# Block 0's loads split over two queues, and the tables, gathers and weight loads around the last blocks reordered, in a retention and mixture-of-experts kernel

## The chip, the cores and the metric

The kernel runs on one core of a Trainium2 chip. The metric is the device time of one execution in microseconds (us), the median of several runs; lower is better. TensorE is called PE here (its weight loads PEld), VectorE is DVE, ScalarE is ACT, GpSimd is POOL and SyncE is SP. DMAs are issued by the queues of SP, ACT and POOL.

## What is computed

The reference has two stages. The first is a retention layer over q, k and v of shape (4, 8, 768, 64); its output, seen as 3072 tokens of 512 numbers, is the input x of the second, a mixture of 8 experts in which each token goes to one expert.

```python
for t in range(S):
    state = gamma[None, :, None, None] * state + np.einsum('bhd,bhe->bhde', k[:, :, t], v[:, :, t])
    y[:, :, t] = scale * np.einsum('bhd,bhde->bhe', q[:, :, t], state)
...
xn = x / (np.linalg.norm(x, axis=-1, keepdims=True) + 1e-06)
en = expert_emb / (np.linalg.norm(expert_emb, axis=-1, keepdims=True) + 1e-06)
logits = xn @ en.T / tau
expert_idx = np.argmax(logits, axis=1)
...
for e in range(E):
    mask = expert_idx == e
    h = np.maximum(x[mask] @ w1[e], 0.0)
    out[mask] = gate_w[mask, None] * (h @ w2[e])
```

## The kernel before

**Blocks.** The retention runs in 12 blocks `m` of 256 tokens. A block's q and k are scaled (`scale_q`, `scale_k`), transposed on PE (`transpose_q`, `transpose_k`), and copied from PSUM by ACT. `scores` makes the products of q and k, `masks` (DVE) takes them out of PSUM, `state` adds k and v to the running state, and `inter` and `intra` make the output; `take` (ACT) copies it, `rows_turn` (DVE) transposes it and `rows` (SP) writes it to the table `xd` in HBM. The order of every engine's instructions is the order of the program text; each queue is in order.

**Start.** Block 0's q comes in two loads and its k in two halves of four heads, all issued by SP (L327, L322). PE meanwhile multiplies zeros (`W0`, L725). DVE scales block 0; later blocks are scaled by POOL.

**Routing.** `expert_emb` is a generator of four steps: load the embeddings `em` and `tau`, start the norm, finish it, transpose to `enT`. Its steps are spread over the starts of blocks 0 to 2. From block 3 on, `logits_products` and `logits_rows` make the logits of finished blocks into a tile called `parts`; `em` and the constant tile `none`, which fills the slot table `tbl` (L834), carry the same name and share two buffers with it. The groups of `GROUPS` finish after blocks 2, 5, 7, 8, 10 and 11: `sums`, `choose` and `add_counts` find each token's expert, `count` and `ranks` its slot, and `place` (POOL, L566) writes its row into `tbl`, one indirect DMA for each 128 tokens. `pad` raises the first expert's count after the fourth group.

**Weights.** `load_piece` (SP) loads 512 KB of weights into one of four `raw` buffers, `split_cast` (ACT, L219) makes the high part, and its `low` (DVE, L224) the low part. The first expert's first four pieces are loaded around blocks 8 and 9 (`LOADS`, and two more at the top of block 9, each piece in four DMAs) and split at the end of block 9 and the top of block 10.

**Hand-over.** In block 10 `early_slots` loads the first 288 slots of expert 0, `early_gather` turns them into indices (`indices`, L590) and fetches their rows (L596) into `xge`. After block 11 PE starts the first expert's layer (`run(n)` makes `n` products of it); the last 128 slots of expert 0 are loaded at L937 and fetched into `xr0` (L1081), which `turn_late` transposes (L1094). The other experts follow one by one.

Of the kernel before, what the change touches and what calls it, by code (L numbers as in the profile page):

```python
# [24 lines left out]
P = 128  # L25
# [28 lines left out]
LOADS = (8, 8)  # L54
# [14 lines left out]
W0 = 10  # L69
# [36 lines left out]
def retention_moe(ctx: ExitStack, tc: tile.TileContext, q, k, v, emb, tau, w1, w2, const, const16, out):  # L106
# [213 lines left out]
    def load(dst, src, m, h=slice(0, H)):  # L320
        b, c = divmod(m, NCB)
        return nc.sync.dma_start(out=dst[:, h], in_=src[b, h, c * T2:(c + 1) * T2, :].rearrange("h (p s) d -> p h s d", s=2))  # L322

    def load_q(m):
        b, c = divmod(m, NCB)
        src = q[b, :, c * T2:(c + 1) * T2, :].rearrange("(j a) (t s) d -> a t j (s d)", a=2, s=8)
        return [nc.sync.dma_start(out=qin[m % 3][:, a], in_=src[a]) for a in range(2)]  # L327

    def load_k(m, h=slice(0, H)):
        return load(kin[m % 3], k, m, h)  # L330
# [21 lines left out]
    def copy_k(m, s, ps, copy=nc.scalar.copy):  # L352
        if m not in kTs:
            kTs[m] = ap_.tile([P, KT, 2, 2, 64], F32, name="kT")
        return copy(out=kTs[m][:, :, :, s], in_=ps.rearrange("p (j u c) -> p j u c", j=KT, u=2))  # L355
# [233 lines left out]
    def indices(p, e, c):  # L589
        nc.gpsimd.tensor_scalar(out=gi[:p, e, c], in0=tb[:p, e, c, 0], scalar1=float(NT - 1), scalar2=None, op0=ALU.min)  # L590

    def tokens(p, e, c):
        nc.gpsimd.tensor_copy(out=si[:p, e, c], in_=tb[:p, e, c, 1])

    def gather(xr, n, j, e, at, rows_=NT):
        return nc.gpsimd.indirect_dma_start(  # L596
            out=xr[:n, j, :], out_offset=None, in_=xd[:rows_, :],
            in_offset=bass.IndirectOffsetOnAxis(ap=gi[:n, e, at:at + 1], axis=0),
            bounds_check=rows_ - 1, oob_is_err=False)
# [124 lines left out]
    for _ in range(W0):  # L724
        nc.tensor.matmul(idle, zeros[:, :P], zeros, start=True, stop=True)  # L725
# [13 lines left out]
    nc.gpsimd.memset(none, float(NONE))  # L739
# [22 lines left out]
    for m in range(NM):  # L762
        nxt = m + 1 < NM
        done = last_of.get(m - 1)
        if waiting is not None:
            pr = count(waiting)
            if span(waiting).stop == NBE:
                pad()
            run_all(ranks(waiting, pr))
            ready += range(span(waiting).start, span(waiting).stop)  # L770
        py_of(m)
        if m == NM - 2:
            first, lows = lows, [split_cast(), split_cast()]
            for u in range(2):
                spread_v(m + 1, u)

        for u in range(2):
            o = masks(scores(m, u), u)
            if u == 0:
                i = o[0]  # L780
        n = 2 if m < 7 else 3 if m < 9 else 4
        if m == NM - 2:
            place(ready)
            ready = []
        if m == 0:
            for j in (*load_q(2), load_k(2)):
                after(j, i)
            nc.sync.dma_start(out=cst2, in_=const[:, _C1:])
            nc.sync.dma_start(out=tri, in_=const16)

        if m + 2 < NM:
            for s in range(2):
                after(scale_k(m + 2, s), i)
            for s in range(2):
                after(scale_q(m + 2, s), i)
        if m == 2:
            nc.gpsimd.tensor_copy(out=zt[:, :, :2], in_=C("ids").rearrange("p (n o) -> p n o", o=2))
# [11 lines left out]
        if m == 0:  # L809
            state(0)  # L810
            state_copy(0)
            state_sums(0)
            intra(0, 0)
# [12 lines left out]
        else:  # L826
# [10 lines left out]
            for i in () if m < 3 else (0, 1, 2) if m == 3 else (m - 1,):  # L837
                logits_rows(i, logits_products(i))
            if nxt:
# [7 lines left out]
                transpose_k(m + 1, 1)  # L847
                rows(m - 1, gathered if m == NM - 2 else None)
                if m == NM - 2:
                    for low in first:  # L850
                        low()
                    load_piece(gathered)
                    load_piece(gathered)
                if done is not None:
# [18 lines left out]
        if m == NM - 3:  # L873
            lows = [split_cast(), split_cast()]
# [3 lines left out]
        if m < 3:  # L878
# [56 lines left out]
    load_expert(1)  # L935
    load_expert(2)
# [3 lines left out]
    run(10)  # L940
    split()
# [6 lines left out]
    for _ in range(4):  # L948
        load_piece()
# [130 lines left out]
    indices(P, 0, slice(3, 4))  # L1080
    gather(xr0, P, 0, 0, 3)  # L1081
# [186 lines left out]
    with ExitStack() as cx:  # L1268
# [3 lines left out]
        def expert_rows(e, i):  # L1272
# [10 lines left out]
            nc.vector.tensor_scalar(out=g1, in0=mt[:, :1], scalar1=float(NT - 1), scalar2=None, op0=ALU.min)  # L1283
            nc.vector.tensor_copy(out=s1, in_=mt[:, 1:2])
# [26 lines left out]
        with tc.If(any_over > 0):  # L1311

            none = op.tile([P, SW], F32, name="none")
            nc.gpsimd.memset(none, float(NONE))
# [39 lines left out]
```

## Time and profile before

| | us |
|---|---|
| median of 3 runs (402.48 to 404.23) | 403.92 |
| the profiled execution | 404.24 |
| its span | 402.5 |
| PE busy | 386.1 |
| DVE busy | 254.1 |
| ACT busy | 213.4 |
| POOL busy | 150.9 |

The span runs from the first to the last recorded instruction; 1.7 us of the profiled execution lie outside it. Times in the rows count from the span's start. A stage is told by its start and end on this scale: the blocks run from about 10 to 118 us, the experts from about 120 us to the end.

### The profile page before, as it was taken

The numbers are of one execution on the slowest core, as the hardware profiler recorded it, in microseconds if no ns is written. First come the engines' busy times: TensorE is split into PE (matmuls) and PEld (weight loads), VectorE is DVE, ScalarE is ACT, GpSimd is POOL, SyncE is SP. The second block draws the span as 40 slices with busy tenths as digits, with TensorE's granted clock in tenths as the row PEclk, the third lists the DMA queues.
The fourth block names the chain that finished last, engine by engine and source line by source line (L and its number), as shares of the span: only waits on it lengthen the run. The fifth ranks groups of instructions, "written<-read, shape, count | busy, mean of one in ns | idle before, by whom it ended". The sixth has DMA issues, their size and how long they took to land.

```text
span 402.5 us, 9525 instructions
## 1 busy us (share of the span) xinstructions
PE 386.1 (96%) x3646; PEld 355.2 (88%) x3646; DVE 254.1 (63%) x539; ACT 213.4 (53%) x378; POOL 150.9 (37%) x171
## 2 busy tenths in 40 slices
PE   6999999999899999999999999999999999999993
PEld 3998788887779978999999999999889889999972
DVE  5497867877889638854863864757456456485400
ACT  3575557565945356555544736725665445463410
POOL 2575487687445522402502611420371062001131
PEclk9999999999999999999999999999999999999998
DMA  7899979889448779589879797787888977933121
GB/s 228 262 287 254 277 225 280 235 229 260 104 130 258 234 263 265 161 267 249 266 223 247 241 302 175 246 277 221 236 273 298 190 240 225 246 122 107 31 99 54
DMA packets 88479, 88.41 MB, mean 220 GB/s; under 512 B 10803, under 2 KB 66995, under 8 KB 88424
## 3 DMA queue, kind: packets, MB, share of 16 engines
q1 hardware_dynamic: 83176, 74.60, 65.4%
q0 software_dynamic: 5072, 13.05, 9.6%
q8 instruction: 30, 0.49, 0.5%
q14 instruction: 25, 0.20, 0.2%
q10 hardware_dynamic: 176, 0.07, 0.1%
HBM read 65.01 MB, written 18.79 MB: 208 GB/s over the span
## 4 chain that ended last, share of the span: by engine, by line
PE 62%; DMA 15%; DVE 7%; issue 5%; SPq 5%; POOL 2%; ACT 2%; POOLq 0%; DVEq 0%
PE pst L237 10%; PE b L237 8%; PE py L1024 8%; PE py L237 8%; PE b L1024 5%; DMA xd<-x 5%; PE pst L1024 4%; PE b L1072 4%; PE py L1072 4%; DMA wlo<-in_k_dram 3%; SPq L1036 2%; DVE x L468 2%; PE b L381 2%; DMA xr<-xd,gi 2%; SPq L475 2%
## 5 line engine op out<-in xcount | busy, mean ns | idle before, releaser
L224 DVE TENSOR_TENSOR wlo<-raw,whi 128x1024 fp32r<-128x1024 f32 x64 | 77.8, 1218 | 23.2 <-ACT whi L219 18.3
L1054 POOL DMA_INDIRECT out_dram<-og,si x28 | 29.3, 1047 | 119.0 <-ACT og L1047 84.2
L219 ACT CAST whi<-raw 128x1024 fp32r<-128x1024 f32 x64 | 66.3, 1044 | 4.7 <-DMA raw<-in_moe_w_dram 4.6
L596 POOL DMA_INDIRECT xr<-xd,gi x25 | 29.3, 1171 | 17.5 <-issue 15.1
L401 DVE TENSOR_TENSOR pm<-b,mask 128x512 f32<-128x512 f32 x48 | 29.8, 681 | 8.9 <-PE b L381 8.9
L344 POOL TENSOR_TENSOR hl<-wlo,cst 128x512 f32<-128x512 f32 x22 | 22.6, 1049 | 31.5 <-DMA wlo<-in_k_dram 17.4
L237 PE MATMUL pst<-xl,whi 128*128 128x380 f32 (+7 forms) x96 | 32.1, 335 | 0.0
L237 PE MATMUL pst<-xh,whi 128*128 128x380 f32 (+7 forms) x96 | 32.0, 334 | 0.0
L237 PE MATMUL pst<-xh,wlo 128*128 128x380 f32 (+7 forms) x96 | 32.0, 333 | 0.0
L1005 DVE STREAM_TRANSPOSE xt<-xg 128x384 f32<-128x384 f32 (+1 forms) x28 | 15.7, 578 | 25.8 <-DMA xg<-xs 25.7
L263 POOL TENSOR_TENSOR r<-r,half 128x4 f32<-128x4 f32 (+1 forms) x9 | 8.9, 991 | 54.1 <-DVE r L262 54.1
L566 POOL DMA_INDIRECT tbl<-zt,sloti x24 | 24.2, 1009 | 12.6 <-issue 5.4
L243 ACT ACTIVATE hh<-pst 128x380 fp32r<-128x380 f32 (+7 forms) x24 | 11.6, 485 | 31.6 <-PE pst L237 31.6
L381 PE MATMUL b<-qT,kT 64*128 64x128 f32 x384 | 24.9, 279 | 2.4 <-ACT kT L355 1.5
L1006 ACT CAST xh<-xt 128x408 fp32r<-128x408 f32 (+6 forms) x28 | 14.2, 510 | 24.1 <-DVE xt L1005 23.8
L237 PE MATMUL b<-xh,whi 128*128 128x408 f32 (+7 forms) x80 | 26.7, 334 | 0.0
L237 PE MATMUL b<-xl,whi 128*128 128x408 f32 (+7 forms) x80 | 26.7, 333 | 0.0
L237 PE MATMUL b<-xh,wlo 128*128 128x408 f32 (+7 forms) x80 | 26.6, 332 | 0.0
L237 PE MATMUL py<-xh,whi 128*128 128x288 f32 (+7 forms) x80 | 26.3, 329 | 0.0
L237 PE MATMUL py<-xh,wlo 128*128 128x288 f32 (+7 forms) x80 | 26.2, 328 | 0.0
L237 PE MATMUL py<-xl,whi 128*128 128x288 f32 (+7 forms) x80 | 26.2, 327 | 0.0
L381 PEld LDWEIGHTS b<-qT,kT 64*128 64x128 f32 x384 | 22.5, 188 | 3.9 <-ACT kT L355 2.8
(220 smaller groups left out, 1044.2 us busy)
## 6 DMA issues: line engine op xcount, KB each, us to landing
raw<-in_moe_w_dram SPq DMA_DIRECT2D x60, 512.0 KB, 4.4
whi<-in_q_dram SPq DMA_DIRECT2D x24, 256.0 KB, 4.0
xd<-x SPq DMA_DIRECT2D x48, 128.0 KB, 4.2
wlo<-in_k_dram SPq DMA_DIRECT2D x11, 512.0 KB
xs<-xr SPq DMA_DIRECT2D x6, 768.0 KB, 4.8
whi<-in_v_dram SPq DMA_DIRECT2D x6, 512.0 KB
wlo<-in_v_dram SPq DMA_DIRECT2D x6, 512.0 KB, 6.0
xg<-xs SPq DMA_DIRECT2D x16, 192.0 KB, 4.6
```

What stands on the lines that cost most here:

```text
L219: nc.scalar.copy(out=hv, in_=rv)
L224: eng.tensor_tensor(out=lv, in0=rv, in1=hv.bitcast(F32), op=ALU.subtract)
L237: nc.tensor.matmul(acc[:, :w], a[:, f], x[:, kt, cols], start=(n == 0), stop=(n == 3 * KT - 1))
L344: return eng.tensor_tensor(out=ks_r[:, m % 3, s, h], in0=kin[m % 3][:, h, s], in1=w[:, h], op=ALU.mult)
L381: nc.tensor.matmul(psc[a][:, j], kTs[m][a * D:(a + 1) * D, j, u].rearrange("p s c -> p (s c)"), q_cols(m, a, j, u), start=True, stop=True, ...
L401: o.append(nc.vector.tensor_tensor(out=pm, in0=psc[a], in1=w, op=ALU.mult))
L566: i = nc.gpsimd.indirect_dma_start(out=tbl[:, :], out_offset=bass.IndirectOffsetOnAxis(ap=sloti[:, n:n + 1], axis=0), in_=zt[:, n], in_off ...
L596: return nc.gpsimd.indirect_dma_start(out=xr[:n, j, :], out_offset=None, in_=xd[:rows_, :], in_offset=bass.IndirectOffsetOnAxis(ap=gi[:n, ...
L1005: nc.vector.transpose(out=xt[:, :n], in_=xgs[e][:, :n, kt * Q:(kt + 1) * Q])
L1024: nc.tensor.matmul(acc[:, :c], a[:, f], x[:, kt, :c], start=(n == 0), stop=(n == 3 * FT - 1))
L1054: i = nc.gpsimd.indirect_dma_start(out=out[:, :], out_offset=bass.IndirectOffsetOnAxis(ap=si[:n, e, j:j + 1], axis=0), in_=og[:n, j, :], i ...
L1072: nc.tensor.matmul(acc[:s, :], x[:, kt, at], a, start=(n == 0), stop=(n == 3 * FT - 1))
```

## The change

- q and k of block 0: one half is issued by SP, the other by ACT behind `cst1`, in front of the embedding loads.
- Warming products: 12 in place of 10 at the start, then `fill` adds one, three and one between the transposes of block 0; their bank is `py0`. `copy_k` of block 0 copies each half for itself.
- The embedding chain: all steps after the loads in block 0. The logits begin in block 2 (blocks 0 and 1), then one block each.
- The slot table holds integers; `early_gather` and the gather of `xr0` take their indices from `tb` as loaded, without `indices`. `xr0` is set to zero by POOL first.
- Weight pieces 0 to 3: two at the end of block 7, two at the end of block 8; split at the end of blocks 8 and 9. Their low parts stay in blocks 10 and 11, the first of them earlier in block 10.
- Block 9: `sums`, `choose`, `add_counts` come before the transposes of `rows`. Block 10: `ranks` before `pad`.
- `scale_q` of block 11 moves from block 9 to block 10, behind `place` and in front of the early gather.
- After block 11: the next expert's first two pieces are issued in front of L937 and the slot loads of experts 1 and 2; two follow at the old place, where there were four.

```diff
-LOADS = (8, 8)
+LOADS = (7, 7, 8, 8)
-W0 = 10
+W0 = 12
...
     def early_gather():
-        indices(P, 0, slice(0, 3))
         for j, n in EROWS:
-            i = gather(xge, n, j, 0, j, NBE * P)
+            i = gather(xge, n, j, 0, j, NBE * P, tb[:n, 0, j, :1].bitcast(I32))
         tokens(P, 0, slice(0, 3))
...
-    idle = pt_()
+    idle = bank("py0")
     halves = [slice(0, H // 2), slice(H // 2, H)]
     nc.scalar.dma_start(out=cst1, in_=const[:, :_C1])
-    load_q(0)
-    for h in halves:
-        load_k(0, h)
+    load_q(0, (nc.sync, nc.scalar))
+    for h, eng in zip(halves, (nc.sync, nc.scalar)):
+        load_k(0, h, eng)
...
+    def fill(n):
+        for _ in range(n):
+            nc.tensor.matmul(idle, zeros[:, :P], zeros, start=True, stop=True)
+
+    fill(W0)
...
     transpose_q(0, 1)
+    fill(1)
     kps = [pt_(), pt_()]
     for i, h in enumerate(halves):
+        js = slice(2 * i, 2 * i + 2)
         for s in range(2):
             scale_k(0, s, nc.vector, h)
         for s in range(2):
             turn_k(0, s, kps[s], range(2 * i, 2 * i + 2))
-    copy_k(0, 0, kps[0])
-    copy_k(0, 1, kps[1], nc.vector.tensor_copy)
+        fill(1 if i else 3)
+        copy_k(0, 0, kps[0], js=js)
+        copy_k(0, 1, kps[1], nc.vector.tensor_copy if i else nc.scalar.copy, js)
...
+            run_all(ranks(waiting, pr))
             if span(waiting).stop == NBE:
                 pad()
-            run_all(ranks(waiting, pr))
...
         if m == NM - 2:
-            first, lows = lows, [split_cast(), split_cast()]
...
+        if m == 0:
+            next(emb_steps)
...
             place(ready)
             ready = []
+            for s in range(2):
+                scale_q(m + 1, s)
...
-            for s in range(2):
+            for s in range(2 if m < NM - 3 else 0):
                 after(scale_q(m + 2, s), i)
...
-        if m == NM - 3:
-            load_piece()
-            load_piece()
...
             state_sums(0)
+            next(emb_steps)
...
-            for i in () if m < 3 else (0, 1, 2) if m == 3 else (m - 1,):
+            if m == NM - 2:
+                lows.pop(0)()
+            for i in () if m < 2 else (0, 1) if m == 2 else (m - 1,):
...
+                if m == NM - 3:
+                    z = sums(done)
+                    run_all(choose(done, z))
+                    run_all(add_counts(done))
                 rows(m - 1, gathered if m == NM - 2 else None)
...
         if m == NM - 3:
-            lows = [split_cast(), split_cast()]
+            lows += [split_cast(), split_cast()]
         take(m)
...
+        if m == NM - 4:
+            lows = [split_cast(), split_cast()]
-        if m < 3:
+        if m == 0:
             next(emb_steps)
...
     load_expert(1)
+    load_piece()
+    run(10)
+    split()
+    load_piece()
     load_expert(2)
     nc.sync.dma_start(out=tb[:, 0, 3], in_=tbl[EARLY:CAPS[0], :2 + NE])
     slots(1)
     slots(2)
-    run(10)
-    split()
     run(12)
...
-    for _ in range(4):
-        load_piece()
+    load_piece()
+    load_piece()
...
-    indices(P, 0, slice(3, 4))
-    gather(xr0, P, 0, 0, 3)
+    nc.gpsimd.memset(xr0, 0.0)
+    gather(xr0, P, 0, 0, 3, idx=tb[:, 0, 3, :1].bitcast(I32))
```

## Rows read from the trace of the kernel before

**Rows 1.** The page, part 1: busy us, share of the span, instructions.

```profile
PE 386.1 (96%) x3646; PEld 355.2 (88%) x3646; DVE 254.1 (63%) x539; ACT 213.4 (53%) x378; POOL 150.9 (37%) x171
```

**Rows 2.** Busy time of each engine in stretches of the span; the first line names the columns.

```profile
core 0: us, PE busy (x) PEld busy (x) DVE busy (x) ACT busy (x) POOL busy (x), PEclk, DMA share, GB/s
0.00:10.00 10.00, 6.53 (x30) 3.16 (x32) 5.21 (x9) 3.76 (x6) 2.60 (x19) 1.00 0.80 227
...
143.50:395.00 251.50, 251.50 (x1360) 238.92 (x1361) 147.51 (x290) 130.97 (x230) 65.16 (x67) 1.00 0.73 216
...
84.00:92.00 8.00, 7.55 (x166) 6.58 (x157) 6.24 (x20) 5.48 (x10) 5.96 (x6) 1.00 0.84 245
```

**Rows 3.** PE's waits from 20 to 165 us: total, times, longest.

```profile
PE b L535 <- DVE oh L526: 2.7, 5, 0.7
...
PE py L444 <- DVE vs L394: 0.4, 1, 0.4
```

**Rows 4.** Timeline of the start: start us, us, engine, line, operation, [idle before].

```profile
0.80 1.33 SPq L327 DMA_DIRECT2D whi<-in_q_dram  x2
...
1.25 3.62 PE L725 MATMUL b<-x 128*128 128x512 bf16 x10 [1.25 <-DVE x L706]
...
2.17 1.14 SPq L322 DMA_DIRECT2D wlo<-in_k_dram  x2
...
5.90 1.06 PE L368 MATMUL b<-ident,hh 128*128 128x128 f32 x8 [1.03 <-DVE hh L339]
...
7.20 1.69 PE L350 MATMUL b<-ident,hl 128*128 128x128 f32 x8 [0.23 <-DVE hl L344]
...
7.63 0.76 DVE L344 TENSOR_TENSOR hl<-wlo,cst 128x256 f32<-128x256 f32 x2 [0.15 <-DMA wlo<-in_k_dram]
...
9.76 2.06 PE L381 MATMUL b<-qT,kT 64*128 64x128 f32 x32 [0.88 <-DVE kT L355]
```

**Rows 5.** Timeline of DVE in block 3.

```profile
41.25 1.11 DVE L496 STREAM_TRANSPOSE parts<-b 128x256 f32<-128x256 f32 x3 [1.93 <-DMA tbl<-parts]
```

**Rows 6.** Timeline of SP, POOL, ACT and PE in blocks 8 to 11.

```profile
86.07 0.54 SPq L322 DMA_DIRECT2D wlo<-in_k_dram  x1
...
92.31 8.33 SPq L192 DMA_DIRECT2D raw<-in_moe_w_dram  x16
...
92.53 2.04 POOL L344 TENSOR_TENSOR hl<-wlo,cst 128x512 f32<-128x512 f32 x2 [1.80 <-DMA wlo<-in_k_dram]
...
99.59 0.17 PE L535 MATMUL b<-oh,tri 128*128 128x16 f16 x1 [0.67 <-DVE oh L526]
...
100.22 1.05 ACT L219 CAST whi<-raw 128x1024 fp32r<-128x1024 f32 x1 [0.98 <-DMA raw<-in_moe_w_dram]
...
103.18 0.97 POOL L566 DMA_INDIRECT tbl<-zt,sloti  x1 [0.30 <-issue]
...
106.01 1.04 PE L368 MATMUL b<-ident,hh 128*128 128x128 f32 x8
106.14 2.50 ACT L394 COPY vs<-wlo 64x512 f32<-64x512 f32 x4
...
108.89 0.95 POOL L590 TENSOR_SCALAR gi<-tb 128x3 int32<-128x3 f32 x1 [4.74 <-DMA tb<-tbl]
...
110.83 2.06 PE L381 MATMUL b<-qT,kT 64*128 64x128 f32 x32 [1.45 <-ACT kT L355]
```

**Rows 7.** Timeline of SP, POOL and PE after block 11.

```profile
132.24 0.35 SPq L937 DMA_DIRECT2D tb<-tbl  x1
...
133.98 1.12 POOL L590 TENSOR_SCALAR gi<-tb 128x1 int32<-128x1 f32 x1 [5.57 <-DMA tb<-tbl]
134.06 2.18 SPq L194 DMA_DIRECT2D raw<-in_moe_w_dram  x4
...
135.37 1.14 POOL L596 DMA_INDIRECT xr<-xd,gi  x1 [0.28 <-DMA tb<-tbl]
...
143.47 0.66 PE L1094 MATMUL b<-ident,xr 128*128 128x128 f32 x4 [0.99 <-DMA xr<-xd,gi]
```

More of the change, by code (lines that the diff above doesn't have):

```diff
@@ L318, in retention_moe, with load, load_q, load_k @@
     xge = ap_.tile([P, len(EROWS), DM], F32, name="xge", bufs=1)
-    def load(dst, src, m, h=slice(0, H)):
+    def load(dst, src, m, h=slice(0, H), eng=nc.sync):
         b, c = divmod(m, NCB)
-        return nc.sync.dma_start(out=dst[:, h], in_=src[b, h, c * T2:(c + 1) * T2, :].rearrange("h (p s) d -> p h s d", s=2))
-    def load_q(m):
+        return eng.dma_start(out=dst[:, h], in_=src[b, h, c * T2:(c + 1) * T2, :].rearrange("h (p s) d -> p h s d", s=2))
+    def load_q(m, engs=(nc.sync, nc.sync)):
         b, c = divmod(m, NCB)
         src = q[b, :, c * T2:(c + 1) * T2, :].rearrange("(j a) (t s) d -> a t j (s d)", a=2, s=8)
-        return [nc.sync.dma_start(out=qin[m % 3][:, a], in_=src[a]) for a in range(2)]
-    def load_k(m, h=slice(0, H)):
-        return load(kin[m % 3], k, m, h)
+        return [engs[a].dma_start(out=qin[m % 3][:, a], in_=src[a]) for a in range(2)]
+    def load_k(m, h=slice(0, H), eng=nc.sync):
+        return load(kin[m % 3], k, m, h, eng)
     def load_v(m, h=slice(0, H)):
@@ L350, in turn_k, with copy_k @@
             nc.tensor.transpose(ps[:, j * P:(j + 1) * P], ks_r[:, m % 3, s, 2 * j:2 * j + 2], ident)
-    def copy_k(m, s, ps, copy=nc.scalar.copy):
+    def copy_k(m, s, ps, copy=nc.scalar.copy, js=slice(0, KT)):
         if m not in kTs:
             kTs[m] = ap_.tile([P, KT, 2, 2, 64], F32, name="kT")
-        return copy(out=kTs[m][:, :, :, s], in_=ps.rearrange("p (j u c) -> p j u c", j=KT, u=2))
+        return copy(out=kTs[m][:, js, :, s], in_=ps.rearrange("p (j u c) -> p j u c", j=KT, u=2)[:, js])
     def transpose_k(m, s, copy=nc.scalar.copy):
@@ L723, in retention_moe @@
     make_identity(nc, ident)
-    for _ in range(W0):
-        nc.tensor.matmul(idle, zeros[:, :P], zeros, start=True, stop=True)
+    def fill(n):
+        for _ in range(n):
+            nc.tensor.matmul(idle, zeros[:, :P], zeros, start=True, stop=True)
+    fill(W0)
     nc.gpsimd.memset(mask, 1.0)
@@ L738, in retention_moe @@
     none = ap_.tile([P, NE * FILL // P * SW], F32, name="parts")
-    nc.gpsimd.memset(none, float(NONE))
+    nc.gpsimd.memset(none.bitcast(I32), NONE)
     for s in range(2):
@@ L847, in retention_moe @@
                 transpose_k(m + 1, 1)
+                if m == NM - 3:
+                    z = sums(done)
+                    run_all(choose(done, z))
+                    run_all(add_counts(done))
                 rows(m - 1, gathered if m == NM - 2 else None)
                 if m == NM - 2:
-                    for low in first:
-                        low()
+                    lows.pop(0)()
                     load_piece(gathered)
                     load_piece(gathered)
-                if done is not None:
+                if done is not None and m != NM - 3:
                     z = sums(done)
@@ L1282, in expert_rows @@
             s1 = op.tile([P, 1], I32, name="s1")
-            nc.vector.tensor_scalar(out=g1, in0=mt[:, :1], scalar1=float(NT - 1), scalar2=None, op0=ALU.min)
-            nc.vector.tensor_copy(out=s1, in_=mt[:, 1:2])
+            nc.vector.tensor_scalar(out=g1, in0=mt[:, :1].bitcast(I32), scalar1=float(NT - 1), scalar2=None, op0=ALU.min)
+            nc.vector.tensor_copy(out=s1, in_=mt[:, 1:2].bitcast(I32))
             xg = op.tile([P, 1, DM], F32, name="xg")
@@ L1313, in retention_moe @@
             none = op.tile([P, SW], F32, name="none")
-            nc.gpsimd.memset(none, float(NONE))
+            nc.gpsimd.memset(none.bitcast(I32), NONE)
             nx = op.tile([P, NE], F32, name="nx")
```

10 lines of the change are left out of this document (5 added, 5 removed).

## Prediction

> **What bounds it.** I read the page's busy times first. PE works for 386.1 of 402.5 us [rows 1]; DVE is next with 254.1. An average hides stages, so the view by stretches came second. From 143.5 to 395 us PE is busy for all of 251.5 us [rows 2]: nothing that DVE, ACT, POOL or SP does faster there can help, and the change adds and removes no product there. The reader is to see that whatever the change brings must come from PE's idle time before 143.5 us, and then shifts everything behind it. The waits of PE list that time, third, and the timeline around each wait, fourth, shows what was late. The places are: the start, where PE computes for real from 5.90 us and goes on without a gap only from 9.76 us [rows 4]; five waits for `choose`, 2.7 us in all [rows 3]; 0.4 us for a DVE copy in block 2 [rows 3]; 1.45 us before block 11's scores [rows 6]; 0.99 us for the gather of `xr0` [rows 7]. The whole purse is some 9 us, and the change reaches for parts of it.
>
> **The start.** The chain is: k's second half, issued by SP as the fourth load (2.17 us plus half of 1.14, so about 2.8), lands at 7.63 us, where DVE had waited for it; scaling 0.76 us, PE's transposes, the copy, scores at 9.76 [rows 4]. With the halves on two queues it is third behind `cst1` on ACT, at about 1.9 us by SP's spacing of 0.6 to 0.7 us for an issue (1.33 and 1.14 us for two), an estimate: 0.9 us earlier. The DMA engines are 0.80 busy over the first 10 us, the empty beginning included, at 227 GB/s [rows 2]: they are nearly full while k lands. So the gain in landing lies between nothing (the bytes set it) and some 1.5 us (also what block 0's v no longer takes from k in the queue). I take 0.9. PE sets a floor of its own: eight passes for q's transposes 1.06 us, four products of zeros before and between k's halves and one behind, at 0.36 us each as a mean of the first ten (3.62/10), an upper bound, and k's transposes, about 0.5 us a half [rows 4]: 5.90 + 1.06 + 1.8 + 1.1 = 9.86 with slow products, 9.1 with products at half that. q's second half also moves from second to first in its queue, worth up to 0.3 us at 5.90. The split copies take the 0.88 us wait for the last copy [rows 4] to about half. The sum: scores at 9.0, 0.8 us earlier, bounds 0 and 1.2. The two more products at 1.25 us lie in the idle 1.03 us before 5.90.
>
> The Trainium skill (DMA: Bandwidth & Descriptors, section "Issuing engines are not separate DMA queues") speaks against this edit: DMAs started by several engines share the same 16 DMA engines, and starting them on several saves only the sequencer's time. The share of 0.80 agrees with it. By that rule alone the gain is at most those 0.9 us and may be nothing, which is the second rival below.
>
> **The embedding chain and the logits.** The same work moves to block 0, where DVE has no queue behind its masks; PE's transposes only change place. Blocks 1 and 2 lose that DVE work, so the copy that PE waited 0.4 us for comes earlier, but block 2 gains two logits transposes (1.11/3 us each [rows 5]). I take 0.2 of the 0.4. In block 3 DVE stood 1.93 us because `parts` took the buffer of `none`, whose DMA into `tbl` had not been read out [rows 5]; PE lost some 0.1 us by it. If `parts` now takes the buffer of `em`, released in block 0, the wait is gone. Together 0.3 us, bounds 0 and 0.6.
>
> **Blocks 7 to 11.** Here gains and losses meet. *For:* with pieces 2 and 3 split at the end of block 9, ACT has only the 2.50 us of copies at 106.14 in front of block 11's copies, not two casts besides: the 1.45 us can go. With `choose` in front of the row transposes, the 0.67 us at 99.59 goes, too [rows 6]. *Against:* (a) ACT's casts at the end of block 9 still wait for their weights, in front of `take`, whose output bank `inter` of block 10 needs. Before, ACT waited until 100.22 for the second piece [rows 6]. Pieces 2 and 3 now stand at the place in SP's queue where 0 and 1 stood (16 DMAs in 8.33 us, so 8 in 4.2), with 1 MB more ahead of them. So the 0.67 us saved is spent waiting for `take`. (b) k of block 11 is issued behind those 4.2 us of pieces: 86.07 becomes about 89.5, and it landed 6.5 us after its issue, at 92.53 [rows 6]. 1.05 MB at 245 GB/s is 4.3 us; the engines were idle for 0.16 of 8 us, 1.3 us [rows 2]. So k lands 3 us later, near 95.5 (bounds 93 and 97). Behind it on POOL stand six `place` and now, in front of the gathers, `scale_q` of block 11. Before, POOL went from 92.53 to 104.15 with scale_k, scale_q and six places, 11.6 us [rows 6]. The order is new, the sum is the same, so `scale_q` now ends 11.6 us behind k, near 107.1, and PE wants it at 106.01 [rows 6]. PE's way from there to block 11's scores was 110.83 - 1.45 - 106.01 = 3.4 us, so they start near 110.5. Before, 110.83. I take 0 for the stretch; bounds are 2.1 us gained (both waits gone) and 1.2 lost (k at 97). The gather is a tie: places end at 105, 0.9 us later, 0.95 us of `indices` and 0.28 of wait are gone, and `scale_q` lies in the 4.74 us wait for the slots [rows 6].
>
> **After block 11.** Slots at 132.24, `indices` 133.98 to 135.10, gather at 135.37; SP's four pieces, 2 MB, were issued from 134.06, and the rows came 8.1 us after the gather's start, at 143.47 [rows 7]. Now `indices` is gone (1.4 us from 133.98 to 135.37), and half of the 2 MB is issued before. The zeroing is hidden in POOL's 5.57 us wait. The two early pieces stand in front of the slot load, which could cost it up to 2 us (1 MB is 4 us at the rate of [rows 2], half of it run by then). PE missed the rows by 0.99 us and comes 1 us earlier by the gains above, so 2 us are needed: 1.4 from `indices`, the rest from 1 MB less beside the gather. I take 1.0 gained, bounds 0 and 1.0.
>
> The Trainium skill (DMA: Bandwidth & Descriptors, section "Queues, rings and completion order") says that one queue's descriptors are consumed in ring order on each DMA engine. Then the slot load would wait out most of the early 1 MB; no row here shows it.
>
> **Sum.** 0.8 + 0.3 + 0 + 1.0 = 2.1 us of the profiled 404.24, 402.1. The median of the runs is 0.3 below that execution, so I say 401.8 for the median.
>
> **Rivals.**
> - *Blocks 9 to 11 pay out.* If k of block 11 lands by 93.5, both waits go: 2.1 us more, 399.7. For it: DMA idle time in 84 to 92. Against: the 1.80 us that POOL already waits for that k [rows 6]. Chance 0.2.
> - *The start or the tail does nothing.* The bytes set k's landing, or the slot load waits out the early pieces and PE's wait stays: 0.8 to 1.0 us less, 402.7. For it: 0.80 of DMA share, SP's order. Chance 0.25.
> - *Block 11 starves (slower).* Each us that k lands after 95.8 (110.83 less 11.6 and 3.4) delays `scale_q`, the slot load, the gathers and block 11 by one. It eats the other 2.1 us at 97.9 and makes the kernel 2 us slower at 99.9: 406. Against: it takes twice the delay that 1 MB costs. Chance 0.05.
> - *`parts` still gets the buffer of `none`.* Then the new logits of block 2, one block or some 9 us ahead of 41.25, wait on DVE for the DMA that ended there [rows 5], and the state sums and copies behind them hold PE: some 7 us, 409. Against: `em` is released first now, and the oldest free buffer is what the trace shows being taken. Chance 0.03.
>
> **Numbers.** The forecast has the remaining 0.47, with a range of its own of 400.8 to 402.9. A measurement of this kernel can tell about 0.5% from no change, 2.0 us, so the line is at 401.9, in the middle of the forecast. Faster by more: 0.2 of the first rival and a little over half of the forecast, 0.47. Slower by more: 0.07. Same: 0.46. To leave out no more than 2 in 10 the range reaches to 399.7 and 403.4.
>
> **What would show it.** In the changed profile: scores of block 0 near 9.0 us; L496 in blocks 2 and 3 with no wait for a DMA; POOL's `scale_k` of block 11 some 3 us later against the places of its block; block 11's scores near 109.7 (110.5 less the 1.1 us of shift); no wait, or a smaller one, at the transposes of `xr0`; PE without a gap from there on. The prediction is wrong if k of block 11 lands as early as before, if a new PE wait appears at block 10's q transposes or at `inter`, or if the first products wait for something on ACT, whose table load now stands behind two more issues.

## The result, and the profile after

The changed kernel took 407.89 us, median of 12 runs (407.04 to 408.96), the kernel before 404.1 us in as many: a ratio of 1.009, 95% interval 1.0072 to 1.0108. It is slower, where 401.8 us and a range of 399.7 to 403.4 had been forecast. The profiled execution of after spans 406.6 us, that of before 402.5.

The page of after, part 1 (busy us) and the line of part 2 that gives the granted TensorE clock in 40 slices of 10.2 us each:

```profile
PE 391.3 (96%) x3653; PEld 359.4 (88%) x3653; DVE 253.5 (62%) x539; ACT 214.3 (53%) x380; POOL 152.7 (38%) x170
...
PEclk9999999999689999999999999999999999999998
```

PE is busy for 5.2 us more than in [rows 1] with nearly the same work (seven more products of zeros). Of the 5.2 us, 1.9 lie in the first 10 us, where the products of zeros are (8.39 us busy; 6.53 in [rows 2]). For the rest, a kernel that is busier and later is either doing more or doing it more slowly; the 6 and the 8 in the eleventh and twelfth slices say the second, between 102 and 122 us. PE's waits up to 165 us say what came ahead of it:

```profile
PE py L444 <- ACT yT L460: 3.2, 1, 3.2
PE b L535 <- DVE oh L526: 2.5, 4, 1.1
...
PE py L444 <- ACT yT L463: 0.5, 1, 0.5
```

The first and the third are new: `inter` of block 10 waits for `take` of block 9 (L460 and L463). The wait for L535 [rows 3] is nearly what it was, and those for L381 and L1094 [rows 6, 7] are gone. The timeline of SP, POOL, ACT and PE around block 10, to be read beside [rows 6]:

```profile
82.95 4.45 SPq L192 DMA_DIRECT2D raw<-in_moe_w_dram  x8
...
88.87 1.10 SPq L322 DMA_DIRECT2D wlo<-in_k_dram  x1
...
89.47 2.06 PE L381 MATMUL b<-qT,kT 64*128 64x128 f32 x32
...
95.28 4.92 SPq L192 DMA_DIRECT2D raw<-in_moe_w_dram  x8
...
95.28 2.45 POOL L344 TENSOR_TENSOR hl<-wlo,cst 128x512 f32<-128x512 f32 x2 [5.33 <-DMA wlo<-in_k_dram]
...
98.75 2.88 PE L381 MATMUL b<-qT,kT 64*128 64x128 f32 x32
...
101.23 1.04 ACT L219 CAST whi<-raw 128x1024 fp32r<-128x1024 f32 x1 [4.38 <-DMA raw<-in_moe_w_dram]
103.27 1.04 ACT L219 CAST whi<-raw 128x1024 fp32r<-128x1024 f32 x1 [0.99 <-DMA raw<-in_moe_w_dram]
104.22 0.58 ACT L460 COPY yT<-py 128x512 f32<-128x512 f32 x1
...
104.85 0.69 PE L444 MATMUL py<-qT,s 64*64 64x128 f32 x4 [3.22 <-ACT yT L460]
...
105.58 2.05 POOL L339 TENSOR_TENSOR hh<-whi,cst 128x512 f32<-128x512 f32 x2
...
116.06 2.06 PE L381 MATMUL b<-qT,kT 64*128 64x128 f32 x32
```

The same stretch of PE and ACT before, with the scores of blocks 9 and 10, the first copy of `take` and `inter` of block 10:

```profile
90.25 2.06 PE L381 MATMUL b<-qT,kT 64*128 64x128 f32 x32
...
100.11 2.43 PE L381 MATMUL b<-qT,kT 64*128 64x128 f32 x32
...
101.17 0.58 ACT L460 COPY yT<-py 128x512 f32<-128x512 f32 x1
...
102.47 1.51 PE L444 MATMUL py<-qT,s 64*64 64x128 f32 x30
```

Read the rows of after from the top. The first two pieces (82.95) push everything behind them in SP's queue: k of block 11 from 86.07 to 88.87, the next pieces from 92.31 to 95.28 [rows 6], 3.0 us. ACT's second cast at the end of block 9 goes from 100.22 [rows 6] to 103.27, the same 3.0 us, and `take` stands behind it (104.22; 101.17 before). PE is through with block 10's scores at 101.63 and idles until 104.85. Then comes what the waits do not list. Busy time in three stretches (columns as in [rows 2]: after the busy times the granted clock, the DMA share, GB/s):

```profile
102.00:104.00 2.00, 0.00 (x0) 0.00 (x0) 2.00 (x4) 1.01 (x2) 1.70 (x2) 0.94 0.95 215
104.00:114.00 10.00, 8.65 (x88) 7.25 (x88) 3.87 (x8) 7.35 (x13) 5.84 (x7) 0.50 0.18 41
114.00:116.00 2.00, 2.00 (x34) 1.73 (x32) 1.04 (x1) 1.32 (x3) 1.10 (x2) 1.00 0.58 164
```

Behind the idle time PE works at a granted clock of 0.50, the 1.2 GHz level, for 10 us, and is back at 1.00 after that. Block 10's scores start 1.36 us earlier than before (98.75; 100.11), block 11's 5.23 us later (116.06; 110.83). All of the loss, 6.6 us by these two numbers, lies between them.

The start and the tail did about what was forecast. The start, beside [rows 4]:

```profile
1.93 0.60 ACTq L322 DMA_DIRECT2D wlo<-in_k_dram  x1
...
7.36 0.76 DVE L344 TENSOR_TENSOR hl<-wlo,cst 128x256 f32<-128x256 f32 x2 [0.46 <-DMA wlo<-in_k_dram]
...
9.07 1.14 PE L381 MATMUL b<-qT,kT 64*128 64x128 f32 x14
```

The logits' transposes in block 2, beside [rows 5], wait for PE and no longer for a DMA:

```profile
31.03 0.88 DVE L496 STREAM_TRANSPOSE parts<-b 128x256 f32<-128x256 f32 x2 [0.98 <-PE b L488]
```

The tail, beside [rows 7]: SP, POOL and PE after block 11.

```profile
136.33 1.01 SPq L194 DMA_DIRECT2D raw<-in_moe_w_dram  x2
138.05 0.34 SPq L955 DMA_DIRECT2D tb<-tbl  x1
...
143.06 1.06 POOL L596 DMA_INDIRECT xr<-xd,tb  x1 [4.14 <-DMA tb<-tbl]
...
147.54 0.60 PE L1110 MATMUL b<-ident,xr 128*128 128x128 f32 x4
...
148.77 0.40 PE L1131 MATMUL b<-whi,xh 128*128 128x512 f32 x1
```

The same product of before, its first of that line:

```profile
144.76 0.40 PE L1115 MATMUL b<-whi,xh 128*128 128x512 f32 x1
```

148.77 less 144.76 is 4.0 us, against 5.2 at block 11's scores: the tail gave back 1.2 us. From there on PE has no gap, as before, and the 4.0 us stay to the end.

### The profile page after: what moved, and what is told of

Same layout as the page of the kernel before. It is cut to its first block, busy times and chain, and to the rows that moved or that the text cites. A ratio compares the mean times of both kernels' runs of the same rounds, so it can differ in the third digit from the quotient of the medians.

```text
span 406.6 us, 9546 instructions
## 1 busy us (share of the span) xinstructions
PE 391.3 (96%) x3653; PEld 359.4 (88%) x3653; DVE 253.5 (62%) x539; ACT 214.3 (53%) x380; POOL 152.7 (38%) x170
## 4 chain that ended last, share of the span: by engine, by line
PE 69%; DVE 9%; DMA 7%; issue 6%; SPq 5%; POOL 3%; POOLq 0%; ACTq 0%; DVEq 0%
PE pst L237 11%; PE b L237 9%; PE py L237 8%; PE py L1040 8%; PE b L1040 6%; PE pst L1040 6%; DMA xd<-x 4%; PE b L1088 4%; PE py L1088 4%; SPq L475 3%; DVE vs L394 3%; DVE x L468 3%; PE b L381 2%; SPq L1052 2%; PE py L444 2%
## 5 line engine op out<-in xcount | busy, mean ns | idle before, releaser
L1070 POOL DMA_INDIRECT out_dram<-og,si x28 | 30.2, 1078 | 124.5 <-ACT og L1063 76.6
L401 DVE TENSOR_TENSOR pm<-b,mask 128x512 f32<-128x512 f32 x48 | 29.8, 684 | 12.3 <-PE b L381 12.3
L243 ACT ACTIVATE hh<-pst 128x380 fp32r<-128x380 f32 (+7 forms) x24 | 11.6, 484 | 27.4 <-PE pst L237 27.4
L381 PE MATMUL b<-qT,kT 64*128 64x128 f32 x384 | 25.5, 280 | 0.1
L381 PEld LDWEIGHTS b<-qT,kT 64*128 64x128 f32 x384 | 22.8, 188 | 1.9 <-ACT yT L460 0.7
```

What stands on the lines that cost most here:

```text
L381: nc.tensor.matmul(psc[a][:, j], kTs[m][a * D:(a + 1) * D, j, u].rearrange("p s c -> p (s c)"), q_cols(m, a, j, u), start=True, stop=True, ...
L401: o.append(nc.vector.tensor_tensor(out=pm, in0=psc[a], in1=w, op=ALU.mult))
L1070: i = nc.gpsimd.indirect_dma_start(out=out[:, :], out_offset=bass.IndirectOffsetOnAxis(ap=si[:n, e, j:j + 1], axis=0), in_=og[:n, j, :], i ...
```

## The experiments

**Theory 1.** ScalarE works in order. It stands on casts whose weights now land 3 us later, `take` of block 9 stands behind them, PE idles 3.7 us for it, and the fall of the granted clock behind that idle costs as much again. The rivals are that the place of the loads does harm by itself (A), that the loss is elsewhere in the change (B), that the late k of block 11 costs as well (C), that the rows gathered for the first expert are late next (D, formed for the third series), and that the chip decides (E, formed for the fourth). In the expectations of e5, e8 and e16 the letters A to C stand for other rivals, which are told there.

The kernels ran in five series (the expectations, word for word below, say "call"), each on a chip of its own, and the kernel before ran beside them each time. The kernel before takes about 404 us on two of these chips, as on that of the result, and 409 to 410 us on three. Each chip was met in one series only, so what is called a kind of chip here rests on that time alone. A ratio is always to the kernel before on the same chip, and only ratios of the same kind of chip are set side by side.

| series, kernel before | kernel | median, us | ratio (95%) |
|---|---|---|---|
| 1, 410.28 us | e1, casts behind take | 407.17 | 0.9931 (0.989 to 0.9971) |
| | e2, weights as before | 407.15 | 0.9945 (0.9913 to 0.9976) |
| | e3, weights alone | 412.1 | 1.0051 (1.0031 to 1.007) |
| | e4, fourteen products | 413.08 | 1.0099 (1.0059 to 1.0139) |
| 2, 404.46 us | e5, the changed kernel | 408.26 | 1.0099 (1.0059 to 1.0139) |
| | e6, start and tail | 402.9 | 0.9963 (0.9942 to 0.9984) |
| | e7, ten products | 406.6 | 1.0063 (1.0032 to 1.0094) |
| | e8, all four early | 411.67 | 1.0172 (1.0143 to 1.0201) |
| 3, 410.1 us | e9, as e1 | 406.58 | 0.9938 (0.9903 to 0.9973) |
| | e10, no wait left | 408.88 | 0.9969 (0.9938 to 0.9999) |
| | e11, start alone | 408.78 | 0.9962 (0.9939 to 0.9985) |
| | e12, as e2 | 407.84 | 0.9956 (0.9931 to 0.9982) |
| 4, 409.16 us | e13, the changed kernel | 406.85 | 0.994 (0.9913 to 0.9968) |
| | e14, as e1 | 406.4 | 0.9925 (0.9893 to 0.9957) |
| | e15, as e10 | 407.03 | 0.9956 (0.9928 to 0.9984) |
| | e16, as e3 | 410.35 | 1.0027 (1.0001 to 1.0054) |
| 5, 404.28 us | e17, the kernel before | 403.71 | 0.998 (0.9957 to 1.0003) |
| | e18, as e1 | 405.38 | 1.001 (0.9982 to 1.0039) |

### Series 1: the pieces and the casts

e1 moves the casts of pieces 2 and 3 to the top of block 10; e2 takes the loads and casts of pieces 0 to 3 back to the kernel before; e3 puts only those of the change into the kernel before.

```diff
 e1, on the changed kernel
         if m == NM - 2:
             for u in range(2):
                 spread_v(m + 1, u)
+            lows += [split_cast(), split_cast()]
...
-        if m == NM - 3:
-            lows += [split_cast(), split_cast()]
         take(m)
```

> The changed kernel, but the casts of weight pieces 2 and 3 stand on ACT behind take of block 9 and behind the copies of v for blocks 10 and 11; the loads stay where the change put them. Theory 1 (ACT stands in its queue on pieces that land late, with take behind them, PE idles 3.2 us for it and its granted clock falls to 0.50): the 3.2 us wait of inter for L460 goes and inter starts near 101.7 us; since scale_q of block 11 ended at 107.6, a wait of up to 3 us may move to the q transposes of block 10, and then the clock may fall there; 403 to 406 us. Rival A (the loads' place alone sets it, whoever waits): within 1 us of the changed kernel, 407 to 408.5 us. Rival B (the loss is elsewhere, at the start or after block 11): unchanged, 407.9 us.

> The changed kernel with the loads and the casts of pieces 0 to 3 back at their places of before; all else is changed. Theory 1: no 3.2 us wait at block 10, the granted clock stays at 1.00, and the other parts of the change show their gain: 400.5 to 402.5 us. Rival A: the same. Rival B: it stays at 407 us or more, as the loss came from another part.

> The kernel before with only the loads and casts of pieces 0 to 3 moved as in the change (two at the end of block 7, two at the end of block 8, cast at the end of blocks 8 and 9). Theory 1 and rival A: PE waits 2 to 4 us for take of block 9 and the clock falls behind it; 4 to 7 us slower than before, 408 to 411 us. If the clock does not fall: 405 to 406.5 us. Rival B: within 1 us of before.

Both e1 and e2 are faster than before by 0.5 to 0.7%, and the pieces by themselves (e3) cost 0.5%: the loss looked settled. It was not, since the chip is of the second kind and the changed kernel had not run on it. Nor does the profile of e3 show what was expected: `inter` of block 10 follows its scores (107.17) without a wait for `take`.

e4 was to fill PE's wait with fourteen products that nothing reads, in front of `inter` of block 10.

> The changed kernel with 14 products of 512 columns of ones (3 us at the full clock) between the scores and inter of block 10, into a bank of the rotation, so that PE is busy while ACT waits. The weights still land late, and take is as late as in the changed kernel. If the fall of the granted clock is half of the loss: the clock stays at 1.00 from 104 to 114 us, inter starts near 104.9 us as before and block 11's scores near 111.5 instead of 116.1 us; 403.5 to 405 us. If the wait alone is the loss and the clock costs nothing: 407 to 408.5 us.

It settles nothing. On this chip block 10's scores themselves had gaps until 106.9 us, the products began only behind them, and they held `inter` up until 110.78. e7 repeats it where the wait exists.

### Series 2: the loss again, its two halves, and the second wall

> The changed kernel as it is, on the chip of the next three, so that they can be compared with it. Theory 1 (ScalarE stands on the casts of the late pieces 2 and 3 with take of block 9 behind them, PE idles some 3.2 us in front of inter of block 10, and the granted clock falls behind it): the same wait of 3 us or more and a stretch at a granted clock near 0.50 show again, ratio 1.007 to 1.011. Rival B (the loss was of that chip, not of the kernel): no such wait, ratio 0.995 to 1.003.

As theory 1 has it: the wait is 3.42 us, the clock 0.50 from 105 to 110 us, the ratio 1.0099.

e6 has all of the change but blocks 8 to 11 (of those it keeps one low part, earlier in block 10).

> The kernel before with the change's start, embedding chain, integer table, gathers without indices and tail; blocks 8 to 11 (weight pieces 0 to 3, choose, ranks, scale_q of block 11) as before. Theory 1: all that the change gains lies here, 0.7 us at the start and about 1 us at the tail and some tenths between: ratio 0.993 to 0.997, block 0's scores near 9.1 us, no wait for xr. Rival (the new order in blocks 9 and 10 is what pays in the kernel with the weights as before): ratio 0.998 to 1.001. Rival (start or tail cost something): over 1.002.

0.9963, that is 1.6 us less than before: the gains are real, and they lie outside blocks 8 to 11. Its PE timeline, block 11's scores and the product shown above for the tail:

```profile
110.72 2.06 PE L381 MATMUL b<-qT,kT 64*128 64x128 f32 x32 [1.43 <-ACT kT L355]
...
143.42 0.40 PE L1127 MATMUL b<-whi,xh 128*128 128x512 f32 x1
```

Block 11's scores are 0.1 us earlier than in [rows 6], with the old wait of 1.4 us in front; the tail's product is 1.3 us earlier than before (144.76). Block 0's scores start at 9.40, 0.36 us earlier than in [rows 4], but block 9's at 90.23, as before: in this profile the start's gain is gone by then, and the tail's 1.2 us stay.

e7 leaves the late casts in place and gives PE ten products to do in the meantime.

```diff
         else:
+            if m == NM - 2:
+                busy = pt_()
+                for _ in range(10):
+                    nc.tensor.matmul(busy.rearrange("p (a b) -> p a b", a=4), ones, ones.unsqueeze(1).broadcast_to([P, 4, P]),
+                                     start=True, stop=True)
             inter(m)
```

> The changed kernel with ten products of ones (about 2.2 us at the full clock), which nothing reads, in front of inter of block 10, where PE idled 3.2 us. ScalarE's wait and the end of take of block 9 stay. Theory 1 with the clock: the stretch at 0.50 shrinks or goes, block 11's scores start 2 to 5 us earlier than in the changed kernel of this call, ratio 0.997 to 1.003. If only the idle time itself costs: block 11's scores start as late, ratio as the changed kernel's, 1.007 to 1.012.

Its timeline of ACT and PE:

```profile
103.11 1.05 ACT L219 CAST whi<-raw 128x1024 fp32r<-128x1024 f32 x1 [0.58 <-DMA raw<-in_moe_w_dram]
...
101.95 2.32 PE L837 MATMUL b<-ones 128*128 128x512 f16 x10 [0.21 <-DVE pm L401]
104.70 0.44 PE L444 MATMUL py<-qT,s 64*64 64x128 f32 x4 [0.43 <-ACT yT L460]
105.89 0.98 PE L444 MATMUL py<-qT,s 64*64 64x128 f32 x26 [0.76 <-ACT yT L463]
...
112.20 2.06 PE L381 MATMUL b<-qT,kT 64*128 64x128 f32 x32
```

And its stretch from 104 to 114 us:

```profile
104.00:114.00 10.00, 8.81 (x154) 7.49 (x152) 5.45 (x9) 9.30 (x17) 7.04 (x7) 1.00 0.17 39
```

The casts are as late as before and `inter` starts at the same time as in the changed kernel (104.70; 104.85). But the clock stays at 1.00, 154 products fit where there were 88, and block 11's scores start at 112.20 and no longer at 116.06. From `inter` to those scores, waits taken off, PE needs 7.50 - 0.76 = 6.7 us here and 11.21 - 0.50 = 10.7 us in the changed kernel (in e5, on the chip of e7, 11.03 - 0.50 = 10.5). So the clock is some 4 us of the loss, and the waits are 3.7. The median gives only 1.7 us of it back. Eight of the twelve runs have a granted clock of 0.992 to 0.998 and spans of 402.8 to 406.3 us, like the profiled one (403.3); four have 0.987 to 0.989 and 407.6 to 410.5 us, and where the clock fell in those was not profiled.

e8 loads all four pieces at the end of block 7 (`LOADS = (7, 7, 7, 7)`).

> The changed kernel with all four weight pieces loaded at the end of block 7 (in place of two there and two at the end of block 8). Theory 1: the casts at the end of block 9 find their data, the wait in front of inter of block 10 goes (under 0.7 us), and with it the fall of the clock there; k of block 11 is issued 4 to 5 us later still and lands near 99 to 100, so the wait moves to block 11: scale_q near 111 to 112 us, block 11's scores near 115, ratio 1.003 to 1.010. Rival A (the pieces' late landing does not matter, the casts themselves in front of take do): the wait in front of inter stays at 2 us or more. Rival C (k of block 11 has time to spare): block 11's scores near 110, ratio 0.993 to 0.998.

```profile
110.09 2.08 POOL L339 TENSOR_TENSOR hh<-whi,cst 128x512 f32<-128x512 f32 x2
...
112.22 1.97 PE L368 MATMUL b<-ident,hh 128*128 128x128 f32 x8 [8.33 <-POOL hh L339]
```

The wait for `take` is gone, and PE stands 8.33 us for `scale_q` of block 11: k is issued at 93.82 and scaled from 99.61, and POOL does six `place` before it comes to `scale_q` at 110.09. This is the chain that the prediction called block 11 starving. The kernel is 1.7% slower, a granted clock of 0.50 from 110 to 115 us included.

### Series 3 and 4: the other kind of chip

e9, e12, e14 and e16 repeat e1, e2, e1 and e3; e13 is the changed kernel.

e10 and e15 put k of block 11 in front of all weight pieces again: pieces 0 and 1 are loaded in block 8 behind the `load_v` of block 11 and cast in front of `take` of block 9, pieces 2 and 3 are loaded at the end of block 8 and cast in block 10 behind the copies of block 11. e11 is e6 without the tail.

```diff
 e10, on the changed kernel
-LOADS = (7, 7, 8, 8)
+LOADS = (8, 8)
...
                     after(load_v(m + 3), i)
+                if m == NM - 4:
+                    load_piece()
+                    load_piece()
                 transpose_k(m + 1, 1)
+                if m == NM - 2:
+                    late = [split_cast(), split_cast()]
...
```

> The changed kernel with one edit, the same as in the first call's kernel of this form: ScalarE's casts of pieces 2 and 3 stand behind take of block 9 and spread_v of block 11 and no longer in front of them. Pieces, their loads and every other order are the change's. Theory 1: PE's 3.2 us in front of inter of block 10 and the stretch at the granted clock of 0.50 are gone, block 11's scores near 110.5, ratio 0.991 to 0.997, so that this one place is the whole loss. Rival C (late k of block 11 costs too): PE waits 1 us or more for q or k of block 11, scores at 111.5 or later, ratio 0.997 to 1.002.

> The changed kernel with k of block 11 loaded in front of the weight pieces again: pieces 0 and 1 stand in block 8 behind the loads of block 11 and in front of the rows, pieces 2 and 3 at the end of block 8; 0 and 1 are cast in front of take of block 9, 2 and 3 in block 10 behind the copies of q and k of block 11. Theory 1 (nothing but the place of the pieces and casts spoils the change): no wait for take over 0.5 us, none for the copy of k, block 11's scores at 107.5 to 109, ratio 0.985 to 0.992. Rival D (the rows for the first expert, gathered by GpSimd, are the next to be late): block 11's scores as early, but PE waits 1 to 3 us for xge, ratio 0.992 to 0.997.

> The kernel before with the start's loads on two queues, the filling products, the split copies, the embedding chain in block 0, logits from block 2 and the integer table with early gathers straight from it; blocks 8 to 11 and the tail (the order of pieces and slot loads, the indices of xr) as before. Theory 1: 0.7 to 1.0 us gained, PE's wait of about 1 us for xr stays, ratio 0.997 to 1.000; the kernel with start and tail gains about 1 us more. Rival (the tail gives nothing): ratio as that kernel's, 0.994 to 0.998.

> The changed kernel with the loads and casts of weight pieces 0 to 3 as in the kernel before, the same as in the first call's kernel of this form, on the chip of the other three. Theory 1: all but the pieces pays, also choose in front of the rows and scale_q of block 11 behind place: no wait for take, block 10's scores near 99, block 11's near 109 or earlier, ratio 0.990 to 0.996, better than the kernel with start and tail alone by up to 1 us. Rival (the new order in blocks 9 and 10 gives nothing by itself): ratio as with start and tail alone, 0.995 to 0.998.

All four are faster than before, by 0.3 to 0.6%, and their intervals overlap: this series tells none of them apart. e9 and e12 have the ratio that was expected, but none of the profiles looks as expected: block 11's scores start at 114.70 in e9, at 114.46 in e10 (107.5 to 109 expected, and the ratio missed too) and at 115.78 in e12. e11 has the ratio of its rival, that the tail gives nothing. But here this doesn't speak against the tail: the wait for `xr` is absent with the old tail. The gather starts at 141.20, 5.8 us later than in [rows 7], PE's transposes at 148.51, 5.0 us later, so the rows took at most 7.3 us in place of 8.1; why is not shown.

> The changed kernel as it is, the control of this call, which the two earlier calls with the casts behind take did not have. Theory 1: PE waits 3 us or more for take of block 9 in front of inter of block 10, ratio 1.007 to 1.012 on a chip where the kernel before runs at about 404 us. Rival E (on a chip where the kernel before takes about 410 us, engines stand for other reasons and the late casts are hidden in that): ratio 0.993 to 1.003 there, and the casts behind take gain less than 0.5% against this run.

Here theory 1 fell as a statement on every chip: the changed kernel is faster than before, 0.994. Its own time, 406.85 us, is about 1 us below that on the first kind of chip (407.89, 408.26); it is the kernel before that takes 5 us more here. The timeline of DVE, ACT and PE in it:

```profile
104.35 0.17 DVE L553 TENSOR_TENSOR rs<-b,oh 128x16 f32<-128x16 f32 x1 [2.53 <-PE b L381]
...
104.08 1.04 ACT L219 CAST whi<-raw 128x1024 fp32r<-128x1024 f32 x1 [0.80 <-DMA raw<-in_moe_w_dram]
105.03 0.58 ACT L460 COPY yT<-py 128x512 f32<-128x512 f32 x1
105.64 1.17 ACT L463 COPY yT<-py 64x512 f32<-64x512 f32 x2
...
104.58 2.54 PE L381 MATMUL b<-qT,kT 64*128 64x128 f32 x16 [1.34 <-DVE rs L553]
107.04 1.98 PE L444 MATMUL py<-qT,s 64*64 64x128 f32 x32
```

The casts are just as late (second one at 104.08), but block 10's scores, begun at 100.67, have gaps in which PE and DVE each seem to wait for the other, by the releasers named. But the products that L553 reads had ended at 100.6 (L535), and two gaps of PE, 0.23 us each, have no releaser at all. The scores end at 107.1; `take` is over at 106.8, and `inter` waits for nothing. The clock falls to 0.50 from 105 to 110 us all the same. The late casts are covered by a stall that chips of this kind seem to have anyway: e11, on the chip of series 3, whose blocks 8 to 11 are nearly those of before, has a like one (block 10's scores from 101.86 to 107.3, clock 0.67 from 105 to 110). Not all that differs lies there: in e13 block 9's scores start at 90.91, 1.4 us later than on the chip of the result (89.47).

> The changed kernel with the casts of pieces 2 and 3 behind take of block 9 and spread_v of block 11, and nothing else different. Theory 1: 1% to 1.6% less than the changed kernel of this call, ratio to the kernel before 0.993 to 0.998 as in the calls on the other chips, block 11's scores 5 us earlier than there, granted clock at 1.00 through blocks 10 and 11. Rival C (k of block 11 lands late as well, so block 11 waits in its turn): within 0.5% of the changed kernel.

> The version with pieces 0 and 1 loaded behind k of block 11 and cast in front of take of block 9, pieces 2 and 3 cast behind the copies of block 11. Theory 1: the fastest of this call, 0.5 to 2 us less than the casts moved, ratio 0.985 to 0.994, block 11's scores at 107.5 to 109.5. Rival D (the rows gathered for the first expert are late next): PE waits 1 to 3 us for xge and the time is that of the casts moved.

> The kernel before with only the loads and casts of weight pieces 0 to 3 as in the change (scale_q of block 11 stays in front of the places, choose behind the rows). Theory 1: this part alone makes the loss, a wait of 2 to 4 us for take of block 9 and a fall of the granted clock behind it, ratio 1.008 to 1.018. Rival B (the loss needs scale_q of block 11 behind the places as well): no more than 1 us of wait in front of inter of block 10, ratio 0.998 to 1.004.

Moving the casts gains little beside e13 (0.9925 and 0.994, overlapping), as rival E says; e15, forecast as the fastest, gains nothing over it. e16 waits for `take` no more than 0.4 us, its clock falls in the same place, and its ratio is the one that its rival B names. Since the stall covers `take` here, that tells nothing on the first kind of chip.

### Series 5: the undo on a chip of the first kind

> The kernel before as it is, to have its profile on this chip. On a chip where it takes about 404 us: the waits of its first profile (1.5 us for the copy of k of block 11, 1.0 us for xr, granted clock 0.99 or more). On a chip where it takes about 410 us, Rival E says that the difference lies in blocks 8 to 11: PE, DVE and ScalarE stand together for nothing that the profile shows between 100 and 108 us, with a fall of the granted clock behind it; if instead the experts (143.5 us to the end) are longer, Rival E falls. Ratio 0.998 to 1.002 on either.

> The changed kernel with the casts of pieces 2 and 3 behind take of block 9 and spread_v of block 11. Theory 1, on a chip where the kernel before takes about 404 us (the changed kernel had 1.009 and 1.010 there): ratio 0.993 to 0.999, no wait for take over 1 us, granted clock 0.99 or more. Rival C (late k of block 11 costs as much): 1.003 or more. On a chip where the kernel before takes about 410 us: 0.992 to 0.995 as before.

The chip was one of 404 us, so e17 says nothing on rival E; it repeats the first profile. In e18 POOL and PE show:

```profile
96.89 2.04 POOL L344 TENSOR_TENSOR hl<-wlo,cst 128x512 f32<-128x512 f32 x2 [7.03 <-DVE wmn L524]
...
107.12 2.06 POOL L339 TENSOR_TENSOR hh<-whi,cst 128x512 f32<-128x512 f32 x2
...
101.83 1.10 PE L444 MATMUL py<-qT,s 64*64 64x128 f32 x32
...
109.23 1.97 PE L368 MATMUL b<-ident,hh 128*128 128x128 f32 x8 [4.21 <-POOL hh L339]
...
114.54 2.06 PE L381 MATMUL b<-qT,kT 64*128 64x128 f32 x32
```

`inter` no longer waits (101.83, straight behind the scores), so the undo does what theory 1 says of the wait, and 1.009 and 1.0099 become 1.001. That lies between what theory 1 and rival C had forecast; the profile, of one of the slower executions (406.81 us; median 405.38), tells more. PE then stands 4.21 us for `scale_q` of block 11, the clock falls to 0.65 from 105 to 110 us, and block 11's scores are still 3.7 us later than in [rows 6]. Rival C holds beside theory 1: one shift of some 3 us in SP's queue made two things late, and the first hid the second.

## Why the prediction was wrong

The step that failed is the term of nothing for blocks 7 to 11, in its part (a). There the prediction put pieces 2 and 3 "at the place in SP's queue where 0 and 1 stood" and let only the 0.67 us be spent waiting for `take`. In part (b) it charged the very same megabyte in front with 3 us for k of block 11. The pieces stand behind k in that queue, so the 3 us were theirs as well: 95.28 against 92.31 at the issue, 103.27 against 100.22 at the second cast. PE, 1.36 us earlier by then, met `take` 3.7 us late, its two waits together, and the clock, of which no step spoke, made it 7.7. This new wait at `inter` is one of the signs by which the prediction said that it would be wrong. Against the loss stand the 1.45 us that block 11's copies no longer cost [rows 6].

Point by point:
- *The bound* was right: PE has no gap behind 143.5 us in either kernel, and all that happened lies ahead of it.
- *The start*, 0.8 forecast, gave 0.69 us (9.07 against 9.76), by another division. k's second half came 0.27 us earlier and not 0.9 (7.36 against 7.63 [rows 4]), though its issue came about 0.9 us earlier (1.93 against some 2.8): most of the landing was set by something else, presumably the bytes. The Trainium skill (DMA: Bandwidth & Descriptors, section "Issuing engines are not separate DMA queues") says that starting DMAs on several engines saves only the sequencer's time. The trace agrees: the gain is less than that time. The other 0.42 us came between k's landing and the scores, where the wait for the last copy went. q's transposes, hoped for up to 0.3 us earlier, came 0.19 later (6.09; 5.90). A slip that changes little: with products at half price the floor adds up to 8.96, not 9.1.
- *The logits*, 0.3 forecast with the embedding chain, gave about 0.1: at block 9's scores PE is 0.78 us ahead (89.47; 90.25), 0.69 of it from the start. The wait of [rows 5] is gone, and the rival in which it stays did not come.
- *The order in blocks 9 and 10* gave the other 0.58 us of the 1.36 by which block 10's scores came earlier; 0.67 was forecast.
- *k of block 11* was scaled from 95.28, forecast 95.5, and `scale_q` ended at 107.6, forecast 107.1. So the chain was right to about half a microsecond, but the wait for it, 1.1 us in the forecast (107.1 less 106.01), was priced as idle time only. In e18, where nothing hides it, k is scaled from 96.89 and PE stands from 105.0 to 109.2. The rival priced at 0.05 charges 1 us for each us of k behind 95.8, so 1.1 us here; block 11's scores came 3.7 us later than before. POOL needed 12.3 us in place of the 11.6, and PE 5.3 us in place of the 3.4, at a granted clock of 0.61. (A slip: 110.5 less the 1.1 us of shift is 109.4, not 109.7; and 86.07 and 4.2 us of pieces are 90.3, not 89.5.)
- *The tail*, 1.0 forecast, gave 1.2. The slot load did wait: it came about 5.0 us after its issue (138.05 to 143.06) and 1.7 us before [rows 7]. The Trainium skill (DMA: Bandwidth & Descriptors, section "Queues, rings and completion order") has the descriptors of one queue taken in ring order on each DMA engine. These two numbers agree with it. PE had enough to do to hide the wait.
- *The sum* of the parts that gained was 2.1 us; e6, which is these parts, measured 1.6 us (0.9963).
- Two rivals were slower than before, 406 and 409 us, and the measured time lies between them. Neither is what happened here: PE stood for `take`, not for `scale_q` of block 11, and DVE didn't wait for the DMA out of `none`.
- On the chip of series 4 the changed kernel reaches 0.994, close to the forecast's 401.8 / 403.92 = 0.995. This doesn't save the step: the kernel before is slower there, and the wait for `take` is covered by a stall of another origin.

What stays open: why PE and DVE, and in some profiles ACT, stall around 102 to 105 us on the chips of 409 to 410 us (no profile of the kernel before was had on one, and whether instructions came late there is untested); and what e2 (the weights as before), e3 (the weights alone) and e10 (k in front again) are worth on a chip of 404 us, since they ran only on the others. So on the first kind the loss is traced to blocks 8 to 11 by e6 and to the casts in front of `take` by e18; that the pieces alone make it was not measured there. Of what ran there, e6 is the best version, 0.4% faster than the kernel before.

## What to carry to other kernels

When a load is put in front in an in-order queue, add its issue time to everything behind it there, one by one, and look up for each what waits for it; here one shift of 3 us reached k and the next pieces, and only one of the two was charged. A cast that waits for a late load belongs behind the copies that TensorE needs, not in front of them; then look for what is late next. And a gain upstream makes every later deadline earlier by the same amount: a transfer that was just in time becomes a wait.

## What the runs showed of the hardware

- An idle time of 3.2 us cost PE more behind it than in itself: 10 us at a granted clock of 0.50 (1.2 GHz), in which it was busy for 8.65 us (from 106.04 to 114 us for all of 7.96 us), some 4 us lost. With the idle broken up by ten products (waits of 0.43 and 0.76 us left) the clock stayed at 1.00.
- The same kernel before takes 404 us in some series and 409 to 410 us in others, each on another chip, at mean granted clocks of 0.993 to 0.998 over its runs of series 2 and 0.982 to 0.997 over those of series 4. The changed kernel takes 408.26 and 406.85 us in these two, so that it is 1% slower in the one and 0.6% faster in the other.
